# An attention, two networks and their fillers: one PSUM tile for the dummy matmuls, gate logits and held expert work beside the attention

## The chip, the cores and the metric

The kernel runs on one core of a Trainium2 chip. The metric is the device time in microseconds (us), median of several runs. The core's engines run side by side, each through its own list of instructions in order: TensorE (PE; its weight loads are PEld), VectorE (DVE), ScalarE (ACT), GpSimd (POOL) and SyncE (SP), which here issues the DMAs. The order of each list is fixed when the kernel is built; on the chip an instruction waits until its operands and its output's place are free.

## The reference

Three stages follow one another. A linear attention with a state per head (4 batches, 8 heads, 768 tokens, 40 channels):

```python
for t in range(S):
    y[:, :, t] = einsum('bhd,bhde->bhe', rt, state)
    Sa = einsum('bhde,bhe->bhd', state, at)
    state = state * wt[:, :, None, :] - einsum('bhd,bhe->bhde', Sa, bt)
    state = state + einsum('bhd,bhe->bhde', vt, kt)
```

Its output, as x of 3072 tokens by 320, goes through 8 experts with 1024 hidden units, weighted by gates that eight Sinkhorn rounds balance over all tokens:

```python
logits = x @ w_gate
P = exp(logits - logits.max())
for _ in range(8):
    P /= P.sum(1, keepdims=True) + 1e-09
    P /= P.sum(0, keepdims=True) + 1e-09
    P *= N / E
out = sum(P[:, e:e+1] * (maximum(x @ w1[e], 0) @ w2[e]) for e in range(E))
```

A last network follows: `h = maximum(maximum(x @ w1, x @ w2), x @ w3)`, `h @ w_out`. All in float32.

## The kernel before

**Attention.** The 768 tokens are six blocks j of 128; a block and a batch b make one of 24 units n. In a unit, products on PE (`products`, L343) give matrices that VectorE masks (L415) or ScalarE copies (`lab_grams`, L364 and L365). The four `lab` matrices of a block are transposed (L374) and inverted by VectorE and GpSimd (`invert`); `chain` then solves a unit in seven steps (L502, L494), each a group of small matmuls and a copy by ScalarE. `post` forms the output `yps` (L541), updates the state and writes to DRAM (`ydr`). After the fourth unit of a block, `inputs` reads it back as x and splits it into a high and a low part (`split_x`, L198 to L201).

**Fill work.** `fill` puts expert 0's first half of the hidden units beside the attention, for five of the six blocks: four layer-1 blocks of 8 matmuls (f) and four layer-2 blocks of 12 (t), in halves, with the sums sent to DRAM (`part0`). It has one PSUM bank (`psf`), so each block waits for the eviction of the one before. Of the fifth block, the layer-2 blocks t = 2 and 3 are held until the last unit's `post` is done (L618).

**Order.** `drive` writes the order of all engines out by hand when the kernel is built. It takes segments (`Seg`: cost on PE, weight w for its activity, engine that follows, what it needs, a gate) from ten flows, keeps its own clock for each engine, and gives PE the first segment that is ready, or fill work where the attention is behind its pace, or dummies: `idle` issues matmuls of `ones` by `ones` (L690) where PE would have nothing to do, planned at 0.22 us each. Each dummy asks `psf` for a tile of its own, and there is one bank: so each waits for the one before it.

**Networks.** `networks` then runs over 16 pieces (expert, half) and six x blocks, the fifth and sixth block first (`order`). `step` is called between blocks of matmuls, and moves the first of two queues each time: `sides` (here `logits`, which makes the gate logits of all six x blocks, and then `sinkhorn`), and `loads` (here `rest`: weights of piece 1, then five loads of the sums from `part0`; then `rest_x`, the four remaining x blocks).

## Time and profile before

| | |
|---|---|
| Median of 3 runs | 2259.83 us (2259.65 to 2262.43) |
| Profiled execution | 2280.62 us, span 2278.9 us |
| PE busy | 98% of the span |
| VectorE, ScalarE, GpSimd busy | 47%, 27%, 13% |
| Last `yps` of the attention | 647.67 us |
| First matmul of the networks | 663.26 us |

All numbers of the trace come from the profiled execution, which took longer than the median by 20.8 us. In rows of a timeline stand the start, the time until the end, the engine, the line, the operation, output and inputs, and how many records it merges (a float32 matmul makes two); a bracket at the end is the engine's idle time before it and the instruction it waited for. PEclk is the granted clock of TensorE as a share of 2.4 GHz.

### The profile page before, as it was taken

Reading aid. Unit: us, or ns where it says so; the run is one execution under the profiler, and the core shown is the slowest. Engines: PE = TensorE matmul, PEld = TensorE weight load, DVE = VectorE, ACT = ScalarE, POOL = GpSimd, SP = SyncE. Lnnn points to the kernel's source line nnn. Section 1 sums busy time; section 2 is a strip of 40 time slices with the busy share of each in tenths; the row PEclk is TensorE's granted clock in tenths of the full one; section 3 lists DMA queues with packets and bytes.
Section 4 is the critical chain, followed back from the end, with each engine's and each line's share of the span. In section 5 each row is a group of like instructions: output and inputs, shape, how many; then the busy total and the mean of one; then the engine's idle time right before and its main releaser. Section 6 shows DMA issues by size and latency. Waiting matters only on the chain.

```text
span 2278.9 us, 37482 instructions
## 1 busy us (share of the span) xinstructions
PE 2240.8 (98%) x16021; PEld 1965.6 (86%) x16021; DVE 1078.1 (47%) x1882; ACT 608.8 (27%) x1223; POOL 286.6 (13%) x455
## 2 busy tenths in 40 slices
PE   9999999999989999999999999999999999999999
PEld 6787888888867989989989999999999989988888
DVE  5545666654324655555555443333343343442332
ACT  3223544443223133122122121121121121222221
POOL 3242545525000001111100000000000000000000
PEclk9997999999999999999999999999999999999999
DMA  4113343422223011111011000000000000100000
GB/s 114 37 46 103 101 123 84 113 71 87 78 77 122 5 35 48 43 36 51 23 48 52 25 26 13 14 26 13 14 26 8 19 27 7 55 6 24 12 12 25
DMA packets 70980, 105.39 MB, mean 46 GB/s; under 512 B 7341, under 2 KB 51117, under 8 KB 70805
## 3 DMA queue, kind: packets, MB, share of 16 engines
q1 hardware_dynamic: 70805, 102.92, 15.8%
q8 instruction: 127, 2.08, 0.4%
q14 instruction: 48, 0.39, 0.1%
HBM read 87.81 MB, written 15.07 MB: 45 GB/s over the span
## 4 chain that ended last, share of the span: by engine, by line
PE 86%; DVE 1%; DMA 1%; ACT 1%; issue 0%; SPq 0%; ACTq 0%; DVEq 0%
PE ps L223 31%; PE ps L215 29%; PE pu L215 9%; PE psg L343 3%; PE z L502 2%; PE yps L541 2%; PE z L494 2%; PE fps L223 2%; PE fps L215 2%; PE z L470 1%; DMA xr<-ydr 1%; PE dps L556 1%; PE z L454 1%; PE yps L529 1%; PE gps L215 0%
## 5 line engine op out<-in xcount | busy, mean ns | idle before, releaser
L223 PE MATMUL ps<-w2h,h 128*128 128x320 f32 x2912 | 656.3, 309 | 0.0
L223 PEld LDWEIGHTS ps<-w2h,h 128*128 128x128 f32 x2912 | 490.6, 188 | 4.4 <-issue 0.3
L226 ACT ACTIVATE h<-ps 128x512 fp32r<-128x512 f32 x364 | 217.9, 599 | 962.5 <-PE ps L215 955.7
L223 PE MATMUL ps<-w2l,h 128*128 128x320 f32 x1456 | 449.5, 309 | 0.0
L227 DVE SCALAR_TENSOR_TENSOR h<-ps,h 128x512 fp32r<-128x512 f32 x364 | 251.4, 692 | 412.7 <-ACT h L226 411.9
L215 PE MATMUL ps<-xh,w1l 128*128 128x512 f32 x1092 | 314.2, 396 | 8.3 <-DVE xh L201 8.3
L215 PE MATMUL ps<-xh,w1h 128*128 128x512 f32 x1092 | 310.4, 392 | 0.0
L1027 DVE SCALAR_TENSOR_TENSOR acc<-ps,lg,acc 128x320 f32<-128x320 f32 x336 | 184.9, 550 | 256.1 <-PE ps L223 254.6
L223 PEld LDWEIGHTS ps<-w2l,h 128*128 128x128 f32 x1456 | 273.2, 188 | 3.7
L215 PEld LDWEIGHTS ps<-xh,w1h 128*128 128x128 f32 x1092 | 205.7, 188 | 46.2
L215 PEld LDWEIGHTS ps<-xh,w1l 128*128 128x128 f32 x1092 | 201.3, 188 | 47.7 <-DVE xh L201 8.6
L215 PE MATMUL ps<-xl,w1h 128*128 128x512 f32 x728 | 227.4, 394 | 0.0
L215 PE MATMUL pu<-xh,uq 128*128 128x512 f32 x648 | 171.2, 394 | 0.0
L215 PEld LDWEIGHTS ps<-xl,w1h 128*128 128x128 f32 x728 | 137.2, 188 | 32.5
L215 PEld LDWEIGHTS pu<-xh,uq 128*128 128x128 f32 x648 | 120.3, 188 | 25.2
L415 DVE TENSOR_TENSOR gr<-psg,mask 128x512 f32<-128x512 f32 x144 | 92.7, 686 | 80.4 <-PE psg L343 79.8
L396 POOL TENSOR_TENSOR tmp<-lt,tt 128x87 f32<-128x87 f32 (+24 forms) x186 | 105.0, 565 | 174.7 <-DVE lt L374 160.6
L135 POOL TENSOR_TENSOR f<-f,m 128x384 f32<-128x384 f32 (+2 forms) x24 | 24.3, 1014 | 680.3 <-DVE m L133 405.6
L690 PE MATMUL spare<-ones 128*128 128x128 f32 x272 | 101.5, 473 | 8.1 <-DVE ones L81 1.1
L400 POOL TENSOR_TENSOR tt<-tt,tmp 128x87 f32<-128x87 f32 (+24 forms) x186 | 106.8, 574 | 14.6
L690 PEld LDWEIGHTS spare<-ones 128*128 128x128 f32 x272 | 63.9, 291 | 42.1 <-PE spare L690 37.6
L1088 DVE TENSOR_TENSOR g<-pu,g 128x512 f32<-128x512 f32 x72 | 49.8, 692 | 99.9 <-PE pu L215 99.9
(171 smaller groups left out, 2435.9 us busy)
## 6 DMA issues: line engine op xcount, KB each, us to landing
e<-in_em_dram SPq DMA_DIRECT2D x23, 626.0 KB
r<-in_moe_w_dram SPq DMA_DIRECT2D x32, 320.0 KB
r<-in_moe_w_dram SPq DMA_DIRECT2D x32, 256.0 KB
bk<-in_tm_dram SPq DMA_DIRECT2D x24, 320.0 KB
xr<-ydr SPq DMA_DIRECT2D x10, 512.0 KB
kr<-in_em_dram SPq DMA_DIRECT2D x24, 208.0 KB
vt<-in_em_dram SPq DMA_DIRECT2D x24, 208.0 KB
r<-in_em_dram SPq DMA_DIRECT2D x24, 208.0 KB
```

What stands on the lines that cost most here:

```text
L215: nc.tensor.matmul(ps, lhsT=a, rhs=b, start=(n == 0), stop=(n == len(seq) - 1))
L223: nc.tensor.matmul(ps, lhsT=a, rhs=b, start=(n == 0), stop=(n == len(seq) - 1))
L226: nc.scalar.activation(out=h[:, 0], in_=ps, func=AF.Relu)
L227: nc.vector.scalar_tensor_tensor(out=h[:, 1], in0=ps, scalar=0.0, in1=h[:, 0].bitcast(F32), op0=ALU.max, op1=ALU.subtract)
L343: nc.tensor.matmul(ps[a][:, q, :], lhsT=lhs[r, q, :], rhs=rhs[r, q, :], start=(q == 0), stop=True, skip_group_check=True, tile_position=(6 ...
L396: eng.tensor_tensor(out=t, in0=lt[:, m:m + 1, m + 1:32].to_broadcast([128, n, w]), in1=tt[:, 0:n, m:m + 1].to_broadcast([128, n, w]), op=A ...
L400: eng.tensor_tensor(out=tt[:, 0:n, m + 1:32], in0=tt[:, 0:n, m + 1:32], in1=t, op=ALU.subtract)
L415: nc.vector.tensor_tensor(out=t, in0=ps, in1=mask.unsqueeze(1).to_broadcast([C, HP, C]), op=ALU.mult)
L494: nc.tensor.matmul(zh[r, h, 0:D], lhsT=lab[0:32 * i, hx(h), 32 * i - 32:32 * i], rhs=u[0:32 * i, h, 0:D], start=False, stop=True, skip_gro ...
L690: nc.tensor.matmul(ps, lhsT=ones, rhs=ones, start=True, stop=True)
L1027: nc.vector.scalar_tensor_tensor(out=acc[:, i], in0=ps, scalar=pr[:, i, e:e + 1], in1=acc[:, i], op0=ALU.mult, op1=ALU.add,)
L1088: nc.vector.tensor_tensor(out=g, in0=ps, in1=g, op=ALU.max)
```

## The change

1. `idle` asks for a PSUM tile only if it has none (`idler`), and all dummies until the next fill block write to that one.
2. `fill` makes the gate logits of its x block ahead of the layer-1 blocks, in the same bank; `logits` in the networks is left with the sixth x block (the second in `order`). The transposes and the copy of the logits are a function, `turn_logits`.
3. The gate that holds work of the fifth block moves from layer-2 blocks t = 2, 3 to layer-1 blocks f = 2, 3; all layer-2 blocks come after those, so two layer-1 and four layer-2 blocks are held instead of two layer-2 blocks.
4. `rest` loads sums and x blocks in turn (the sums of the first block in `order`, then x and sums of each of the last four), where before all five sums came ahead of the x blocks.

```diff
--- before.py
+++ after.py
@@ -227,6 +227,11 @@
         nc.vector.scalar_tensor_tensor(
             out=h[:, 1], in0=ps, scalar=0.0, in1=h[:, 0].bitcast(F32), op0=ALU.max, op1=ALU.subtract
         )
+
+    def turn_logits(tps, lt, j):
+        for t in range(4):
+            nc.tensor.transpose(tps[:, t, :], lt[:, t * 128:t * 128 + 128], ident[0:NE, 0:NE])
+        nc.vector.tensor_copy(lg[:, 4 * j:4 * j + 4, :], tps)
 
     def load_gate(p):
         wg = p.tile([128, 3, NE], F32, name="wg")
@@ -599,8 +604,19 @@
                 yield Seg(gate=lambda: len(xf) > j)
                 x, x_ = xf[j]
                 hs = []
+                g = Seg(pe=1.87, eng="A", cost=0.65, needs=[bank, x_])
+                yield g
+                idler.clear()
+                ps = psf.tile([NE, TB], F32, tag="f", name="gps")
+                mm_in(ps, *gate, slice(0, NE), x)
+                lt = chp.tile([NE, TB], F32, tag="yt", name="lgt")
+                nc.scalar.activation(out=lt, in_=ps, func=AF.Copy)
+                bank = Seg(pe=0.35, eng="V", cost=0.2, needs=[g])
+                yield bank
+                turn_logits(psf.tile([128, 4, NE], F32, tag="f", name="tps"), lt, j)
                 for f in range(4):
-                    yield Seg(pe=0.92, needs=[bank, x_])
+                    yield Seg(pe=0.92, needs=[bank, x_], gate=lambda: j < NJ - 2 or f < 2 or count["post"] == units)
+                    idler.clear()
                     fs = slice(f * 128, f * 128 + 128)
                     ps = psf.tile([128, TB], F32, tag="f", name="fps")
                     mm_in(ps, ws[0]["h1"], ws[0]["l1"], fs, x, slice(0, 4))
@@ -615,7 +631,8 @@
                     hs.append(h)
                     count["done"] += 1
                 for t in range(4):
-                    yield Seg(pe=0.88, needs=[bank], gate=lambda: j < NJ - 2 or t < 2 or count["post"] == units)
+                    yield Seg(pe=0.88, needs=[bank])
+                    idler.clear()
                     ps = psf.tile([128, TB], F32, tag="f", name="fps")[:, 0:DM]
                     layer2(ps, ws[0]["2"], hs, t, slice(0, 6))
                     spare.append(None)
@@ -686,8 +703,9 @@
         def idle(n):
 
             for _ in range(n):
-                ps = psf.tile([128, 128], F32, tag="f", name="spare")
-                nc.tensor.matmul(ps, lhsT=ones, rhs=ones, start=True, stop=True)
+                if not idler:
+                    idler.append(psf.tile([128, 128], F32, tag="f", name="spare"))
+                nc.tensor.matmul(idler[0], lhsT=ones, rhs=ones, start=True, stop=True)
                 spend(0.22, 1.0)
 
         def behind():
@@ -741,7 +759,7 @@
                     take(f)
 
         with tc.manual_schedule():
-            spare = []
+            spare, idler = [], []
             mask = k0.tile([C, C], F32, name="mask")
             ends = k0.tile([128, WC], F32, name="ends")
             wmid = k0.tile([HR, 1], F32, name="wmid")
@@ -940,7 +958,7 @@
                 yield
 
         def logits():
-            for j in range(NJ):
+            for j in range(1 if begun else 0, 2 if begun else NJ):
                 while len(xs) <= j:
                     yield
                 yield
@@ -950,10 +968,7 @@
                 lt = sm.tile([NE, TB], F32, tag="lt", name="lgt")
                 nc.scalar.activation(out=lt, in_=ps, func=AF.Copy)
                 yield
-                tps = pss.tile([128, 4, NE], F32, tag="s", name="tps")
-                for t in range(4):
-                    nc.tensor.transpose(tps[:, t, :], lt[:, t * 128:t * 128 + 128], ident[0:NE, 0:NE])
-                nc.vector.tensor_copy(lg[:, 4 * order[j]:4 * order[j] + 4, :], tps)
+                turn_logits(pss.tile([128, 4, NE], F32, tag="s", name="tps"), lt, order[j])
 
         pr = lg
 
@@ -1104,18 +1119,25 @@
                 step()
 
         with tc.manual_schedule():
+            def rest():
+                yield from staged(piece(ws[1], wp[1], rp, *pieces[1], "r"), 1)
+                ready.append(1)
+                for k in range(NJ):
+                    if k > 1:
+                        r = fetch_x(rp, order[k])
+                    if k != 1:
+                        nc.sync.dma_start(out=acc[:, 4 * order[k]:4 * order[k] + 4], in_=part0[order[k]])
+                    yield
+                    if k > 1:
+                        for _ in range(3):
+                            yield
+                        xs.append(load_x(xp, r))
+
             def rest_x():
                 yield from staged([
-                    (lambda j=j: fetch_x(rp, order[j]), lambda r, j=j: xs.append(load_x(xp if j or begun else xa, r)))
-                    for j in range(2 if begun else 0, NJ)
+                    (lambda j=j: fetch_x(rp, order[j]), lambda r, j=j: xs.append(load_x(xp if j else xa, r)))
+                    for j in range(NJ)
                 ], 1)
-
-            def rest():
-                yield from staged(piece(ws[1], wp[1], rp, *pieces[1], "r"), 1)
-                for j in order[:1] + order[2:]:
-                    nc.sync.dma_start(out=acc[:, 4 * j:4 * j + 4], in_=part0[j])
-                ready.append(1)
-                yield
 
             ready = []
             if begun:
@@ -1125,7 +1147,7 @@
                 xs = []
                 for load, use in piece(ws[0], wa, rp, *pieces[0], "r"):
                     use(load())
-            loads.append(rest_x())
+                loads.append(rest_x())
             sides.extend((logits(), sinkhorn()))
             prev = None
             last = len(pieces) - 1
```

Rows of the order, as built. First PE at the start of the attention, up to the fifth product of `at` and `bt` (the first of unit 4); `spare` is the dummies' tile, and a name with a number in the brackets is the semaphore of the engine waited for. Before:

```order
L343 MATMUL psg<-at,bt_152 128x128 [waits DVE_49,Activation_49]
L343 MATMUL psg<-at,bt_152 128x128 [waits Activation_49]
L343 MATMUL psg<-at,bt_152 128x128 x6
L690 MATMUL spare<-ones 128x128 [waits PE_49] x9
L343 MATMUL psg<-at,bt 128x128 [waits DVE_49,Activation_49]
L343 MATMUL psg<-at,bt 128x128 [waits Activation_49]
L343 MATMUL psg<-at,bt 128x128 x6
L690 MATMUL spare<-ones 128x128 [waits PE_49] x47
L343 MATMUL psg<-at,bt 128x128 [waits DVE_49,Activation_49]
```

Now:

```order
L348 MATMUL psg<-at,bt_152 128x128 [waits DVE_49,PE_49,Activation_49]
L348 MATMUL psg<-at,bt_152 128x128 [waits PE_49,Activation_49]
L348 MATMUL psg<-at,bt_152 128x128 x6
L708 MATMUL spare<-ones 128x128 x9
L348 MATMUL psg<-at,bt 128x128 [waits DVE_49,PE_49,Activation_49]
L348 MATMUL psg<-at,bt 128x128 [waits PE_49,Activation_49]
L348 MATMUL psg<-at,bt 128x128 x6
L708 MATMUL spare<-ones 128x128 x47
L348 MATMUL psg<-at,bt 128x128 [waits DVE_49,PE_49,Activation_49]
```

The sequence and the counts are the same; the dummies' wait for PE is gone, and the products have one for PE. In the whole program 136 dummies become 167: the first 125 stand in the same places, up to the sixth unit's chain.

Second, PE at the end of the attention, from the last output `yps`; `fps` is the fill's bank, `ps_` that of the networks' first layer-1 block, which reads the sixth x block. Before:

```order
L541 MATMUL yps<-gr,kb 40x128 x8
L223 MATMUL fps<-w2h,fh 128x320
...
L223 MATMUL fps<-w2h,fh 128x320
L690 MATMUL spare<-ones 128x128 x3
L223 MATMUL fps<-w2h,fh 128x320
...
L223 MATMUL fps<-w2h,fh 128x320
L215 MATMUL ps_7028<-xh,w1l 128x512 x3
L215 MATMUL ps_7028<-xl,w1h 128x512 x2
```

Now:

```order
L546 MATMUL yps<-gr,kb 40x128 x8
L215 MATMUL fps<-xh,w1l 128x512 x3
...
L708 MATMUL spare<-ones 128x128 x8
L215 MATMUL fps<-xh,w1l 128x512 x3
...
L708 MATMUL spare<-ones 128x128 x8
L223 MATMUL fps<-w2h,fh 128x320
...
L223 MATMUL fps<-w2h,fh 128x320
L215 MATMUL ps_7017<-xh,w1l 128x512 x3
L708 MATMUL spare<-ones 128x128 x3
L215 MATMUL ps_7017<-xl,w1h 128x512
L223 MATMUL fps<-w2h,fh 128x320
```

Two layer-1 blocks and one layer-2 block now stand ahead of the first matmul on the sixth x block; the other three layer-2 blocks stand between that matmul and its followers, each behind 3 dummies. In the last two units 15 dummies stand where there were 8 (with 3 more, above, behind `yps`).

Third, SP's queue at the change of stage; `part_72` to `part_76` are the sums of blocks 1 to 5, `ydr_66` to `ydr_69` the x of blocks 1 to 4. Before:

```order
L1116 DMA acc<-part_76 128x1280
L1116 DMA acc<-part_72 128x1280
L1116 DMA acc<-part_73 128x1280
L1116 DMA acc<-part_74 128x1280
L1116 DMA acc<-part_75 128x1280
L193 DMA xr<-ydr_66 128x2x512
L194 DMA xr<-ydr_66 64x512
L193 DMA xr<-ydr_67 128x2x512
```

Now:

```order
L1129 DMA acc<-part_76 128x1280
L193 DMA xr<-ydr_66 128x2x512
L194 DMA xr<-ydr_66 64x512
L1129 DMA acc<-part_72 128x1280
L193 DMA xr<-ydr_67 128x2x512
L194 DMA xr<-ydr_67 64x512
L1129 DMA acc<-part_73 128x1280
```

The x of the first block stands behind one load of sums instead of five.

## Rows read from the trace of the kernel before

**Rows 1.** Page, part 1: busy time, share of the span, instructions.
```profile
PE 2240.8 (98%) x16021; PEld 1965.6 (86%) x16021; DVE 1078.1 (47%) x1882; ACT 608.8 (27%) x1223; POOL 286.6 (13%) x455
```

**Rows 2.** Stretches: us, busy of PE, PEld, DVE, ACT, POOL, PEclk, DMA, GB/s.
```profile
94.00:162.00 68.00, 67.31 (x527) 56.32 (x526) 28.53 (x47) 21.56 (x58) 17.46 (x31) 1.00 0.23 58
162.00:231.00 69.00, 65.10 (x791) 55.07 (x790) 41.03 (x69) 27.68 (x69) 20.48 (x34) 0.83 0.36 97
231.00:648.00 417.00, 411.27 (x5639) 359.25 (x5637) 232.78 (x374) 167.01 (x405) 161.37 (x254) 1.00 0.33 91
```

**Rows 3.** Tile of the dummies: ns min/median/max; waits for the dummy before.
```profile
L690 PE MATMUL spare<-ones x272: 275/421/582, 1.1 to 652.6; 128*128 128x128 f32 x136
...
  PE spare L690: 37.6, 111
```

**Rows 4.** Stretches, dummies alone: us, PE and PEld busy, PEclk, DMA.
```profile
0.00:94.00 94.00, 71.58 (x180) 45.15 (x180) 1.00 0.31 77
94.00:162.00 68.00, 14.99 (x39) 9.61 (x38) 1.00 0.23 58
162.00:231.00 69.00, 9.53 (x32) 5.86 (x32) 0.83 0.36 97
```

**Rows 5.** Timeline of PE at the start: start us, us, what, records.
```profile
39.06 2.08 PE L343 MATMUL psg<-at,bt 64*128 64x128 f32 x16
...
56.43 24.69 PE L690 MATMUL spare<-ones 128*128 128x128 f32 x58
...
81.05 2.08 PE L343 MATMUL psg<-at,bt 64*128 64x128 f32 x16
...
89.97 3.47 PE L470 MATMUL z<-v,gr 128*128 128x40 f32 x16
...
93.96 1.27 PE L502 MATMUL z<-zs,td 32*32 32x40 f32 x16
...
114.26 5.06 PE L690 MATMUL spare<-ones 128*128 128x128 f32 x12
```

**Rows 6.** Timeline of DVE, operands of the products at the start.
```profile
15.71 0.69 DVE L329 TENSOR_TENSOR at<-e,p 128x512 f32<-128x512 f32 x1
...
24.55 0.68 DVE L329 TENSOR_TENSOR at<-e,p 128x512 f32<-128x512 f32 x1
...
69.12 0.71 DVE L329 TENSOR_TENSOR at<-e,p 128x512 f32<-128x512 f32 x1
...
72.98 0.68 DVE L428 TENSOR_TENSOR kt<-kr,ip 128x512 f32<-128x512 f32 x1
```

**Rows 7.** Timeline of PE, two products of rows 5 at the faster pace.
```profile
183.79 1.88 PE L470 MATMUL z<-v,gr 128*128 128x40 f32 x16
...
225.88 1.16 PE L343 MATMUL psg<-at,kt 64*128 64x128 f32 x16
```

**Rows 8.** Timeline of ACT, the copy before L502 at 119.3 us.
```profile
114.48 0.43 ACT L498 ACTIVATE zs<-z 32x320 f32<-32x320 f32 x1
```

**Rows 9.** Timeline of PE, end of the attention and start of the networks.
```profile
647.67 1.07 PE L541 MATMUL yps<-gr,kb 128*40 128x128 f32 x16
...
663.26 1.65 PE L215 MATMUL ps<-xh,w1l 128*128 128x512 f32 x3 [8.32 <-DVE xh L201]
...
677.16 0.86 PE L215 MATMUL gps<-xh,gl 128*8 128x512 f32 x3 [1.17 <-DVE lg L956]
...
696.87 1.44 PE L215 MATMUL gps<-xh,gl 128*8 128x512 f32 x3 [5.47 <-DVE xh L201]
```

**Rows 10.** Chain that ended last, same place: start us, us, what.
```profile
652.91 2.04 PE fps L223 x12
...
671.91 1.87 PE gps L215 x8
...
681.05 12.62 DMA xr<-ydr
...
696.87 3.50 PE gps L215 x8
```

## The prediction

> **What bounds the kernel now.** I read the engine shares first: TensorE (PE) is busy for 98% of the profiled span [rows 1]. So only three things can move the end: PE time that is no work, PE idle time, and work done at the lower of TensorE's two clock levels. The table by stretches shows where such time is left. From 231 to 648 us, the attention with expert work beside it, PE is busy for 411 of 417 us at a granted clock of 1.00. From 162 to 231 us the granted clock is 0.83 [rows 2]. Before 162 us the column says 1.00, yet the durations say otherwise: eight products L343 take 2.08 us there and 1.16 us at 226 us, eight products L470 3.47 us at 90 us and 1.88 us at 184 us [rows 5, 7]. I go by the durations: up to about 166 us PE works at 1.2 GHz, later mostly at 2.4 GHz.
>
> Next I looked at the dummies. The view of their tile counts 272 records, two for each of 136 dummies, and 111 waits of a dummy's weight load for the dummy before it, 37.6 us in all [rows 3]. By stretch the dummies hold PE for 71.6, 15.0 and 9.5 us, 96 of 101 us before 231 us [rows 4]. The timeline at the start shows what this does: 47 dummies stand between the product at 39.06 us and that at 81.05 us, 0.85 us each (24.69 us for 29), while VectorE had the operand of the latter ready at 69.8 us [rows 5, 6]. Last I read the change of stage: PE waits 8.3 us for the last x, then 1.2 us and 5.5 us near gate logits [rows 9].
>
> **Part A, the start, up to the first step of the chain (L502, 93.96 us).** With one shared tile a dummy no longer waits for its predecessor (the order loses these waits; the counts up to the sixth unit, 125 dummies, are unchanged). No row shows a 128x128 dummy without the wait. From below I take L470, also a 128x128 stationary operand in two records: 3.47/8 = 0.43 us at the low level, 1.88/8 = 0.235 us at the high one [rows 5, 7]; from above the 0.85 us of today. L470 moves only 40 columns, but it is the nearest row and I take it. At the low level: second product at 16.4 us (operand at 15.71 + 0.69), 2.0 us long; 8 dummies, 3.4 us; third product at 21.9; 9 dummies, 3.9 us; fourth at 27.8 us, not 39.06: 11.3 us earlier, and its operand is there at 25.2 [rows 6]. ScalarE, VectorE and GpSimd follow that product, so the operand at 69.8 comes at 58.5 us. The 47 dummies end at 29.8 + 20.2 = 50.0 us and block nothing; what is late next is VectorE. The product starts at 58.5 instead of 81.05; the next one, on kt, waits 1.0 us for kt (73.66 - 11.3 = 62.4 us). That is 21.5 us, and the 5 dummies before 93.96 give 5 x 0.42 = 2.1: **24 us**. At the high level the fourth product starts at 25.2 us, the products are shorter, and it comes to 29. What rows 3 show is what the Trainium skill describes in "TensorE: Matmul & The Clock Gate", "A second HAM failure mode: psum-queue depth-cycling": going from one PSUM buffer to the next leaves short PE idles, and the clock moves between its levels. The trace agrees with the idles (111 of them); the same page speaks against this change as well, below.
>
> **Part B, from there to 231 us.** 19 dummies stand in 94 to 162 us, 16 in 162 to 231 us. They cost 15.0 and 9.5 us [rows 4]; at 0.43 us each 8.2 and 6.9, at 0.235 us 4.5 and 3.8. That saves 9 to 16 us, and I take 12. These dummies stand where PE waits for the chain, so part of that is lost when they get shorter: before L502 at 119.3 us the six take 5.06 us, but ScalarE's copy is done at 114.9 us, so 4.3 us are pure delay [rows 5, 8]. Then the clock: 67.3 - 15.0 = 52.3 us of PE work runs low in 94 to 162 us [rows 2, 4]; at the high level it would take 1.16/2.08 of that, 23 us less. Nothing shows whether denser dummies lift it; between 0 and 23 I take 10, since PE will now also stand idle between steps. B is **22 us**, bounds 9 and 39.
>
> **Part C, expert work in the attention.** Five of six gate logits go from the network into the attention, each 8 matmuls of 1.87 us [rows 10] and four small transposes; PE is full on both sides, so 9 us leave one and enter the other: 0. If cover is missing, PE waits for ScalarE's copy of them.
>
> **Part D, end of the attention.** The last yps ends at 648.67 us and x is usable at 663.26, 14.6 us later [rows 9]; the chain ydr to xr to split does not change. Before, two layer-2 blocks (2.0 us each [rows 10]) lie in that gap; now the order puts two layer-1 blocks, 16 dummies and one layer-2 block there, and then the matmul that needs x: 5.7 us of work instead of 4.0. PE still waits 14.6 - 5.7 - 16 x 0.235 = 5 us. The other three layer-2 blocks follow with 9 dummies (2.1 us), and 7 more dummies stand in the last two units (1.6 us), where the held work was. 1.7 - 2.1 - 1.6 = **-2 us**.
>
> **Part E, start of the network.** The waits of 1.17 and 5.47 us belong to logits that are gone from here. The second was for the third x, whose DMA took 12.6 us behind five loads of sums on SP's queue [rows 9, 10]; the logits after it took 3.50 us, 1.6 more than at the high level. SP now has one load of sums ahead of that x, and PE needs it only after more than 40 us of other matmuls: 8.2 us go. The Sinkhorn starts at once behind the last logits, and three small PE instructions wait for VectorE with everything queued behind them. Nearest row: 1.17 us each, 3.5 us (bounds 0 and 8). **+5 us**.
>
> **Sum.** 24 + 22 - 2 + 5 = 49 us. The profiled execution took 2280.6 us (span 2278.9), so its like would take 2232. The median of the runs is 2259.8, 20.8 less. Taking the extra as spread evenly, the forecast is 2259.8 - 49 = **2211 us**. If it lay wholly in the stretch before 231 us, the gain would be 28 and the time 2232.
>
> **Rivals.**
> 1. The clock rises early and stays up: A 29, B 39, so 29 + 39 - 2 + 5 = 71 us and 2189 us. For it: back-to-back dummies are dense work, and the matmuls that follow one another from 663 us on start at 1.65 us for three and are at 1.87 us for eight 9 us later [rows 9, 10]. Against: PE will idle from 50.0 to 58.5 us. The Trainium skill, "TensorE: Matmul & The Clock Gate", "What's actually happening", has activity release the throttle, which is this case.
> 2. The clock stays low to 162 us and the chain's own waits (ScalarE's copies, kr's loads) take most of the dummies' place: A 24, B 2, D and E 3: 29 us, 2231 us. For it: after idles of 8.3 and 5.5 us the trace has PE slow each time [rows 9]. The same page, "HAM oscillation — how this bites in real kernels", says idle gaps between bursts put PE back to the low clock: a rule against a change that shortens fillers. By it B's clock part is 0.
> 3. A dummy still waits for the last write to its tile: A and B are 0, and +3 is left: 2257 us. Against: the waits are gone from the order.
> 4. Slower: PE falls to the low level between 231 and 648 us, because a logits block holds the only spare bank through two copies and the fills come too late. Each us of high-level work would take 0.79 us more (2.08/1.16); from 49/0.79 = 62 us of the 411 on, the gain is eaten, and at a quarter, 103 us, the time is 2259.8 - 49 + 81 = 2292 us. For it: 0.83 in 162 to 231 us. Against: 1.00 over all of the stretch, which gets more work [rows 2].
>
> **How the numbers follow.** Forecast 0.58, rivals 0.16, 0.18, 0.04, 0.04. The forecast's own range is 2198 to 2227, B's bounds mostly. To leave out no more than 2 in 10 the range takes most of rivals 1 and 2: 2188 to 2238. What this kernel's measurement tells from no change is about 0.2% (4.5 us): faster than that 0.92, within it 0.04, slower 0.04.
>
> **What would show it.** Right: dummies of 0.5 us or less at the start; the fifth product of at and bt near 58 us with VectorE as its releaser; the first L502 chain step (now L507) near 70 us; no 5.5 us wait behind the network's first layer 2; about 5 us of wait for the last x. Wrong: dummies of 0.85 us; PE busy short of 95% with the attention's end not earlier than 625 us; a granted clock under 0.9 after 231 us.

## The result, and the profile of the changed kernel

| | before | changed |
|---|---|---|
| Median | 2260.07 us (2259.65 to 2262.43, 4 runs) | 2232.46 us (2231.34 to 2233.89, 4 runs) |
| Ratio, 95% interval | | 0.9876 [0.9859, 0.9893] |
| Profiled execution | 2280.62 us | 2231.34 us |
| The same pair later, beside the experiments | 2264.09 us (17 runs) | 2230.87 us (6 runs), 0.9846 [0.9802, 0.9891] |

The change gains 27.6 us by the medians. The two profiled executions lie 49.3 us apart, because the profiled execution of before was a long one. Rows of the changed kernel follow the order of the rows of before; its lines behind L229 are 5 to 18 numbers later (L507 was L502, L475 L470, L348 L343, L315 L310, L708 L690).

The page's busy line, the answer to [rows 1]:

```profile
PE 2172.6 (97%) x16083; PEld 1930.9 (87%) x16083; DVE 1082.4 (49%) x1882; ACT 609.5 (27%) x1223; POOL 284.0 (13%) x455
```

PE has 68 us less busy time with 31 more dummies. The stretches of [rows 2], same columns:

```profile
94.00:162.00 68.00, 62.68 (x784) 53.74 (x781) 39.17 (x64) 27.11 (x69) 39.36 (x62) 0.77 0.37 95
162.00:231.00 69.00, 65.84 (x898) 56.34 (x898) 50.80 (x81) 28.12 (x68) 33.66 (x49) 0.96 0.39 106
231.00:648.00 417.00, 403.72 (x5204) 347.03 (x5203) 211.52 (x339) 155.87 (x368) 123.84 (x208) 0.98 0.30 84
```

PE runs 784 matmul records between 94 and 162 us where it ran 527. The tile of the dummies, [rows 3], durations in ns:

```profile
L708 PE MATMUL spare<-ones x334: 273/275/583, 1.1 to 634.3; 128*128 128x128 f32 x167
...
  DVE fh L227: 6.5, 4
```

No wait of a dummy for a dummy is left (there were 111); the 6.5 us are new and come up below. The dummies alone, by the stretches of [rows 4]:

```profile
0.00:94.00 94.00, 31.72 (x210) 29.28 (x210) 0.78 0.37 94
94.00:162.00 68.00, 6.80 (x30) 4.96 (x30) 0.77 0.37 95
162.00:231.00 69.00, 1.65 (x10) 1.26 (x10) 0.96 0.39 106
```

40 us instead of 96. PE's timeline at the start, [rows 5]:

```profile
25.37 1.25 PE L348 MATMUL psg<-at,bt 64*128 64x128 f32 x16 [0.96 <-DVE at L334]
26.55 10.76 PE L708 MATMUL spare<-ones 128*128 128x128 f32 x94
55.37 2.17 PE L348 MATMUL psg<-at,bt 64*128 64x128 f32 x16 [18.06 <-DVE at L334]
...
63.17 3.47 PE L475 MATMUL z<-v,gr 128*128 128x40 f32 x16
...
67.16 1.27 PE L507 MATMUL z<-zs,td 32*32 32x40 f32 x16
...
158.85 1.14 PE L459 MATMUL z<-s,at 104*128 104x104 f32 x8
```

The 47 dummies take 10.76 us, 0.23 us each, instead of 40 us; VectorE releases the product at 55.37 us; the chain's first step stands at 67.16 us instead of 93.96. The last row is the first product of unit 4, a mark used below: it came at 207.67 us before.

The end of the attention and the start of the networks, [rows 9]:

```profile
611.71 1.07 PE L546 MATMUL yps<-gr,kb 128*40 128x128 f32 x16
...
616.24 2.05 PE L708 MATMUL spare<-ones 128*128 128x128 f32 x16 [1.41 <-DVE fh L227]
...
621.88 2.05 PE L708 MATMUL spare<-ones 128*128 128x128 f32 x16 [1.41 <-DVE fh L227]
...
645.20 0.27 PE L980 MATMUL t<-ident,m 128*1 128x128 f32 x1 [1.65 <-DVE m L977]
646.03 0.58 PE L986 MATMUL t<-m,ones 1*128 1x1 f32 x2 [0.56 <-DVE m L983]
```

The waits of 8.32, 1.17 and 5.47 us are gone. Two batches of eight dummies stand behind waits of 1.41 us for the only spare bank, and the Sinkhorn brings two waits of its own. One wait is new in the middle. VectorE's timeline, then PE's:

```profile
114.79 0.84 DVE L315 TENSOR_SCALAR e<-e 128x512 f32<-128x512 f32 x1 [5.38 <-DMA e<-in_em_dram]
```

```profile
120.94 1.67 PE L546 MATMUL yps<-gr,kb 128*40 128x128 f32 x8 [3.19 <-DVE gr L420]
...
133.99 1.27 PE L507 MATMUL z<-zs,td 32*32 32x40 f32 x16 [1.32 <-ACT zs L503]
```

PE's granted clock around it (us, PE busy, PEclk, DMA, GB/s):

```profile
110.00:120.00 10.00, 7.69 (x138) 1.00 0.51 122
120.00:130.00 10.00, 9.06 (x92) 0.66 0.51 130
130.00:140.00 10.00, 7.93 (x75) 0.70 0.36 101
140.00:150.00 10.00, 10.00 (x113) 0.50 0.27 66
```

VectorE's list is in order, so the wait for a load holds back the state update and the masked products behind it; PE stands idle for them, and then works mostly at 1.2 GHz up to about 158 us. From 127 to 134 us its steps are at the high level again; the second fall comes with a wait of 1.32 us for ScalarE's copy. The faster kernel has run into its loads: before, the same instruction (unit 9's) waited 1.11 us, at 159.16 us.

**Where the time went.** Each execution is cut at three marks: the chain's first step, unit 4's first product, the start of the last `yps`. Most of the experiments stand here too (us, all from PE's timeline and the span):

| kernel | to first step | to unit 4 | to last `yps` | rest |
|---|---|---|---|---|
| before | 93.96 | 113.71 | 440.00 | 1631.2 |
| before, profiled again | 93.96 | 104.48 | 439.26 | 1630.5 |
| changed | 67.16 | 91.69 | 452.86 | 1617.9 |
| changed, again | 67.14 | 94.65 | 451.88 | 1619.8 |
| shared tile only | 67.13 | 91.60 | 442.18 | 1627.6 |
| all but the shared tile | 75.93 | 105.96 | 454.76 | 1624.2 |
| changed, no dummy issued | 66.72 | 95.21 | 452.69 | 1612.9 |
| before, 35 dummies fewer | 76.26 | 113.66 | 450.91 | 1628.0 |
| shared tile late only | 93.97 | 91.57 | 439.13 | 1629.1 |
| shared tile early only | 67.23 | 101.90 | 447.35 | 1630.3 |
| changed, end trimmed | 67.45 | 91.71 | 448.68 | 1616.1 |
| trimmed, one load counted longer | 65.56 | 76.61 | 456.87 | 1616.6 |
| trimmed, seven loads counted longer | 67.17 | 73.83 | 450.11 | 1616.3 |

Between the two profiled executions the first two columns carry the gain: 26.8 and 22.0 us. The last two exchange about 13 us with each other. The two rows that start at about 76 us have a tile for each dummy at the start, as before; they come up below.

### The profile page after: what moved, and what is told of

Same layout as the page of the kernel before. It is cut to its first block, busy times and chain, and to the rows that moved or that the text cites. A ratio compares the mean times of both kernels' runs of the same rounds, so it can differ in the third digit from the quotient of the medians.

```text
span 2229.6 us, 37611 instructions
## 1 busy us (share of the span) xinstructions
PE 2172.6 (97%) x16083; PEld 1930.9 (87%) x16083; DVE 1082.4 (49%) x1882; ACT 609.5 (27%) x1223; POOL 284.0 (13%) x455
## 4 chain that ended last, share of the span: by engine, by line
PE 89%; ACT 1%; DVE 1%; DMA 0%; issue 0%; SPq 0%; ACTq 0%
PE ps L223 32%; PE ps L215 30%; PE pu L215 9%; PE psg L348 3%; PE z L507 2%; PE yps L546 2%; PE fps L215 2%; PE z L499 2%; PE fps L223 2%; PE z L475 1%; PE dps L561 1%; PE z L459 1%; ACT ld L369 1%; PE yps L534 1%; PE spare L708 1%; PE tp L439 0%
## 5 line engine op out<-in xcount | busy, mean ns | idle before, releaser
L215 PEld LDWEIGHTS ps<-xh,w1l 128*128 128x128 f32 x1092 | 200.9, 188 | 38.5
L507 PEld LDWEIGHTS z<-zs,td 32*32 32x32 f32 x1536 | 63.6, 111 | 23.2 <-issue 9.7
L507 PE MATMUL z<-zs,td 32*32 32x40 f32 x1536 | 75.4, 202 | 5.5 <-ACT zs L503 5.4
```

The costliest lines, as they stand in the source:

```text
L215: nc.tensor.matmul(ps, lhsT=a, rhs=b, start=(n == 0), stop=(n == len(seq) - 1))
L507: nc.tensor.matmul(zh[r, h, 0:D], lhsT=td[r, 8 * b + hx(h), :], rhs=zs[r, h, :], start=(h == 0), stop=True, skip_group_check=True, tile_po ...
```

## The experiments

**The kernel before, once more.** No edit.

> The kernel before, unchanged, for a second profile and the clocks of its runs. Its profiled execution took 2280.6 us, its runs 2260, and the changed kernel gained 49 us between the profiled executions but 28 between the medians. Theory (the extra 20.8 us lie in the start): a profile near 2260 shows the first chain step of the fifth unit (L502) near 200 us instead of 220.5, and the stretch from there to the end unchanged. Rival (spread evenly): 220.5 and all later stretches 1% shorter.

2269.7 us (10 runs) beside 2270.8 (23 runs of before); ratio 1.0015 [0.998, 1.005]. Its profiled execution took 2269.87 us, 10.75 less than the first one, and 9.2 of that lies between the first step and unit 4 (second column). The granted clock of this one:

```profile
160.00:180.00 20.00, 18.62 (x268) 0.97 0.34 91
180.00:200.00 20.00, 19.13 (x236) 0.77 0.36 92
```

In the first profile the rows of these stretches read 0.78 and 0.71. All steps stand at the same times up to 150 us; then the clock rises, at about 155 us here and 168 us there, by the durations of the steps. The fifth unit's first step comes at 211.3 us, and the rest is as long as before: as the theory has it, though the profile lies 10 us from 2260. So one program differs from run to run by when its clock rises; 17 runs of before on one chip reach from 2251 to 2283 us.

**The shared tile alone.** The kernel before with `idler` and nothing else (shown in part; `idler.clear()` stands ahead of each fill block):

```diff
...
+                if not idler:
+                    idler.append(psf.tile([128, 128], F32, tag="f", name="spare"))
+                nc.tensor.matmul(idler[0], lhsT=ones, rhs=ones, start=True, stop=True)
```

> The kernel before with the shared dummy tile alone; fill, logits and loads as before. Theory (the dummies' waits were the cost, parts D and E are worth about 3): 2233 to 2240 us, 20 to 27 of the 28 us gained, first chain step near 67 us. Rival (the end of the attention and the start of the networks carry the gain): 2248 to 2256 us.

2229.69 us (6 runs), ratio 0.9828 [0.9778, 0.9878]. Within the intervals this is all of the change's gain.

**All but the shared tile.** The changed kernel with a tile for each dummy:

```diff
-                if not idler:
-                    idler.append(psf.tile([128, 128], F32, tag="f", name="spare"))
-                nc.tensor.matmul(idler[0], lhsT=ones, rhs=ones, start=True, stop=True)
+                ps = psf.tile([128, 128], F32, tag="f", name="spare")
+                nc.tensor.matmul(ps, lhsT=ones, rhs=ones, start=True, stop=True)
```

> The changed kernel with a tile of its own for each dummy, as before: logits beside the attention, held work and loads in turn are kept. Theory: 2254 to 2262 us, since the start is as before and D and E together are near +3 (more dummies at the end of the attention now wait for one another). Rival: 2235 to 2245 us.

2268.71 us (12 runs), ratio 1.0011 [0.9978, 1.0043]: nothing. But the start is not as before in this profile:

```profile
32.94 1.16 PE L348 MATMUL psg<-at,bt 64*128 64x128 f32 x16
34.03 25.64 PE L707 MATMUL spare<-ones 128*128 128x128 f32 x94
...
75.93 1.27 PE L507 MATMUL z<-zs,td 32*32 32x40 f32 x16
```

The steps turn fast at about 23 us, among dummies that wait for one another; the 47 dummies take 0.55 us each, and the chain starts 18.0 us earlier than in either profile of before. The dummies of this stretch stand as before, on a tile each, so the edit is no likely reason for it: executions with waiting dummies differ at the start too, by the clock. Later the clock is up from 84 to 91 us and then down to about 145 us.

Against the shared tile alone, the changed kernel's third column is 10.7 us longer and its last 9.7 shorter. By PE's busy time 10 us of logits go into the third column and 8 us of held fill work out of it into the last; dummies, waits and the clock make up the rest.

**No dummy issued.** The changed kernel as planned, with no dummy matmul issued:

```diff
-                if not idler:
-                    idler.append(psf.tile([128, 128], F32, tag="f", name="spare"))
-                nc.tensor.matmul(idler[0], lhsT=ones, rhs=ones, start=True, stop=True)
```

> The changed kernel with no dummy issued: they are planned, so the order of all else is the same, and left out. Theory (they hold nothing up any more and keep the clock higher in part): slower than the changed kernel by 5 to 15 us, near 2243, first chain step at about 68 to 70 us and products at 2.08 us up to the fifth unit. Rival (dummies now only cost time): 2215 to 2228 us.

2235.57 us (4 runs), ratio 0.9863 [0.9801, 0.9924], which the changed kernel's ratio can't be told from. Two of its chain steps:

```profile
94.88 1.27 PE L507 MATMUL z<-zs,td 32*32 32x40 f32 x16
...
101.09 0.76 PE L507 MATMUL z<-zs,td 32*32 32x40 f32 x16
```

From about 100 us on they take 0.76 us, the time at the high level, without any dummies, until the clock falls at 120 us as it does in the changed kernel. In the profiles of before they take 1.27 us up to some 155 and 168 us, and with all but the shared tile, in the same order, the granted clock is 0.50 from 100 to 140 us. So in these profiles dummies on a tile each did not merely fail to lift the clock: the rise that lasts came some 45 to 68 us later with them than with none. Neither theory has the time.

**35 of the 47 dummies left out.** The kernel before; the 12 left are on a tile each:

```diff
...
+                if count["lab"] != 4 or count["pre"]:
                     ps = psf.tile([128, 128], F32, tag="f", name="spare")
                     nc.tensor.matmul(ps, lhsT=ones, rhs=ones, start=True, stop=True)
```

> The kernel before, with 35 of the 47 dummies that stand ahead of the fifth product not issued (12 are left, each on its own tile); nothing else is changed and nothing is left out of the result. Theory A (the dummies cost time only because each waits for the one ahead of it, and so stand between ready work and PE): the 12 end near 50 us, the product of 81.05 us starts when VectorE is done (69.8 us, its producer itself held by the product of 39.06 us), so the first step of the chain comes 11 us earlier (83 us) and the run 8 to 14 us under the kernel before. Theory B (the gain of the shared tile is that dense dummies lift the clock): without these dummies the clock has less reason to rise, the chain starts at or after 93.96 us and the time is that of before within 5 us. If the first step comes 11 us earlier and the time does not follow, what is gained at the start is given back by a later rise of the clock.

2268.19 us (12 runs), ratio 1.0007 [0.9979, 1.0036]. The start obeys theory A; the time is theory B's:

```profile
33.23 1.16 PE L343 MATMUL psg<-at,bt 64*128 64x128 f32 x16
...
63.18 2.08 PE L343 MATMUL psg<-at,bt 64*128 64x128 f32 x16 [22.37 <-DVE at L329]
...
76.26 1.27 PE L502 MATMUL z<-zs,td 32*32 32x40 f32 x16
...
330.06 0.41 PE L541 MATMUL yps<-gr,kb 128*40 128x128 f32 x2 [1.72 <-DVE gr L415]
```

The chain starts 17.7 us earlier. But 5.8 us of that are there ahead of the dummies left out: the fourth product comes at 33.23 us instead of 39.06, since the clock was up from about 23 us in this execution, as with all but the shared tile. That is luck of this execution; the other 11.9 us are the 11 of theory A. Against the second profile of before, its second column is 9.2 us longer (the clock is at 0.50 to 150 us, 74 us behind the first step, where that profile took 61) and its third 11.7 us. The clock behind the wait of 1.72 us:

```profile
330.00:340.00 10.00, 9.76 (x112) 0.54 0.27 66
340.00:350.00 10.00, 10.00 (x74) 0.50 0.01 3
350.00:360.00 10.00, 10.00 (x86) 0.76 0.37 107
```

That is 24 us at 1.2 GHz ((0.46 + 0.50 + 0.24) x 10 x 2), or 24 x (1 - 1.16/2.08) = 10.6 us lost. In this profile the earlier start is given back where the clock stays down longer. That is one profile; the twelve runs (2255 to 2273 us) say only that there is no gain.

**The shared tile late, and early.** The kernel before with the shared tile for the dummies behind unit 0's first stage only, and for those ahead of it only (the edit against the shared tile alone):

```diff
-                if not idler:
+                if not idler or not count["pre"]:      # late; early: or count["pre"]
+                    idler.clear()
```

> The kernel before, in which only the dummies planned from the end of unit 0's first stage on (from about 92 us of the profile of before on: 14 batches before 231 us and all later ones) share a tile; the 85 or so ahead of it stay on a tile each. Theory 1 (the clock of the chain decides: dummies that wait for one another keep it low between 94 and 160 us, and the 27 us at the start are worth little by themselves): the chain still starts at 92 to 94 us, but it runs at the high level from about 120 us on, and 15 to 35 us of the 36 to 41 us are kept (2225 to 2250, ratio 0.985 to 0.993). Theory 2 (as predicted: the start carries 24 to 27 us and the rest about 10): 5 to 12 us under before, ratio 0.995 to 0.998.

2246.81 us (12 runs), ratio 0.9908 [0.9879, 0.9937], which is 20.9 us of 2269.4 [14 to 27].

```profile
93.97 1.27 PE L502 MATMUL z<-zs,td 32*32 32x40 f32 x16
...
107.85 0.76 PE L502 MATMUL z<-zs,td 32*32 32x40 f32 x16 [0.75 <-ACT zs L498]
```

The start is as before to 0.01 us, and two steps later the chain runs at the high level. The second column shrinks to 91.57, the value of the changed kernel.

> The other half: only the dummies ahead of the end of unit 0's first stage share a tile, the later ones have a tile each. The chain starts near 67 us, as in the changed kernel. Theory 1 (the clock decides): it then runs at the low level up to 130 us or more and most of the 27 us are lost again, as where 35 of the 47 dummies were left out: 0 to 12 us under before (ratio 0.995 to 1.0). Theory 2 (the start carries it): 24 to 30 us under before, ratio 0.987 to 0.99.

2247.28 us (12 runs), ratio 0.9931 [0.9902, 0.996], which is 15.7 us [9 to 22]. The steps run low for longer again:

```profile
104.67 1.27 PE L502 MATMUL z<-zs,td 32*32 32x40 f32 x16
110.47 0.76 PE L502 MATMUL z<-zs,td 32*32 32x40 f32 x16
...
308.83 0.41 PE L541 MATMUL yps<-gr,kb 128*40 128x128 f32 x2 [1.68 <-DVE gr L415]
```

The start is 26.7 us earlier than in the profiles of before, and about 16 us are gained. The wait of 1.68 us is followed by 20 us at the low level in this profile, and the third column is 8.1 us longer than in the second profile of before; but the other runs of before may have started earlier than its two profiles (see the end), and then there was less to gain. The halves add up: 20.9 + 15.7 = 36.6 us, where the shared tile alone gave 39.1 [28 to 50] and the changed kernel 34.9 [25 to 45]. The late half came out as theory 1 had it; the early half lies between the two theories. Beside the same runs of before the two medians are 0.5 us apart, so which half is worth more is not shown.

**The changed kernel again**, beside the runs with fewer dummies, denser ones and a trimmed end.

> The changed kernel unchanged, beside the others on one chip. If the shared tile carries all of the change and the other parts are worth nothing, it is within 6 us of what the kernel before with the shared tile alone showed against before (ratio 0.983, 0.978 to 0.988). If the profiled pair (gain 49 us) is the rule, the ratio is 0.978 or less; if the medians of the first runs (gain 27.6 us) are, 0.988.

2230.87 us (6 runs), ratio 0.9846 [0.9802, 0.9891]: as the shared tile alone, within its interval.

**Denser dummies.** In the changed kernel, 2 and 3 matmuls by turns for 35 of the 47 planned dummies ahead of the fifth product (shown in part):

```diff
+                for i in range(1 if count["lab"] != 4 or count["pre"] else 2 + count["extra"] % 2):
                     nc.tensor.matmul(idler[0], lhsT=ones, rhs=ones, start=True, stop=True)
```

> The changed kernel, with 2.5 times as many dummies in the stretch ahead of the fifth product (they end near 54 us instead of 37.3, VectorE's operand comes at 55.4), so that PE no longer stands idle for 18 us before it. Theory (the idle 18 us put the clock back to the low level): products 5 and 6 take 1.2 us instead of 2.17 and the first chain steps run high, 4 to 15 us less than the changed kernel. Rival (the clock of the stretch up to 160 us is set by the waits within the chain): the products are faster by 2 us and nothing else moves; the time is that of the changed kernel within 3 us.

2232.67 us (6 runs), ratio 0.9854 [0.981, 0.990]: no gain. The condition leaves 12 of the 47 as they were, so there are 99 dummies and not 2.5 times 47; they end near 49 us instead of 54, PE still idled 6.5 us and the product that follows is still slow:

```profile
27.02 22.38 PE L709 MATMUL spare<-ones 128*128 128x128 f32 x198
55.86 2.17 PE L348 MATMUL psg<-at,bt 64*128 64x128 f32 x16 [6.46 <-DVE at L334]
```

So this run does not tell what a start at the high level would be worth.

**The end trimmed.** The changed kernel without the dummies behind the last unit, and with more turns in the Sinkhorn:

```diff
+                if count["post"] == units:
+                    spend(0.22, 1.0)
+                    continue
...
+            for _ in range(3):      # ahead of t1; one turn more ahead of t2 and of each ct
+                yield
```

> The changed kernel, with the dummies planned behind the last unit of the attention not issued and 2 to 3 more turns ahead of the three small PE instructions of the Sinkhorn. Theory: in the changed kernel 2 x 2.07 us (8 dummies each, behind the release of their bank, so pure delay), up to 3 x 0.76 us of dummies among the held work, and 1.65 + 0.56 + 0.25 us of Sinkhorn waits are PE time that nothing needs: 4 to 9 us less than the changed kernel (it may give 2 us back, since PE then waits for the last x). Rival: the clock falls for want of dummies and the gain is gone: same time, with matmuls at the low level behind 616 us.

2224.49 us (6 runs), ratio 0.9826 [0.9778, 0.9873]; 6 us under the changed kernel beside it, though the two ranges overlap (2220 to 2235, 2228 to 2236). In the profile the two batches of 2.05 us are gone; the turns did not help:

```profile
635.55 0.27 PE L984 MATMUL t<-ident,m 128*1 128x128 f32 x1 [1.65 <-DVE m L980]
639.57 0.58 PE L991 MATMUL t<-m,ones 1*128 1x1 f32 x2 [3.75 <-DVE m L987]
```

The second wait grew from 0.56 to 3.75 us. The cause stays open.

**The load of e counted longer.** The trimmed kernel; `drive` takes 3 us more for the load that VectorE waited for (shown without the trimming):

```diff
+                    if k == 2 * NB + 1:
+                        ready[k] = Seg(done=ready[k].done + 3.0)
```

> The changed kernel without the dummies behind the last unit and with more turns in the Sinkhorn (as in the trimmed run, 6 us under the changed kernel), and with one number of the planner's changed: it counts 3 us more for the load of e for unit 9, so that VectorE's state update of unit 1 and two products with the mask stand ahead of the instruction that waits 5.4 us for that load. Theory: this wait on VectorE's queue is what makes PE stand idle for 3.1 us at 121 us, and with that the clock falls until 150 us: without it 3 us of wait go and up to 13 us of low clock: 6 to 16 us under the trimmed run, ratio to before 0.975 to 0.980. Rival (PE then waits some us later for something else and the clock falls all the same): within 4 us of the trimmed run, ratio 0.981 to 0.985.

2215.80 us (6 runs), ratio 0.9795 [0.9755, 0.9835]. VectorE now does unit 1's state update and two masked products first, and the wait of 5.4 us is 0.2:

```profile
112.39 0.74 DVE L315 TENSOR_SCALAR e<-e 128x512 f32<-128x512 f32 x1 [0.20 <-DMA e<-in_em_dram]
127.85 0.43 DVE L315 TENSOR_SCALAR e<-e 128x512 f32<-128x512 f32 x1 [2.47 <-DMA e<-in_em_dram]
```

PE's clock around it:

```profile
120.00:130.00 10.00, 9.51 (x148) 1.00 0.74 200
130.00:140.00 10.00, 8.69 (x100) 0.74 0.26 65
140.00:150.00 10.00, 10.00 (x73) 0.50 0.42 123
```

The fall comes some 13 us later, behind the load for the next unit. In the table the stretch up to unit 4 is 15 us shorter than in the trimmed run, and the third column 8 us longer. The intervals of the two ratios overlap (0.9826 [0.9778, 0.9873] for the trimmed run), so a gain in time against it is not shown. So I counted all loads of units 9 to 15 longer (`2 * NB + 1 <= k < 4 * NB`).

> As the last run, but the planner counts 3 us more for the loads of e of units 9 to 15, not of unit 9 alone. In the last run the load for unit 10 became the next wait: VectorE waited 2.5 us for it at 127.9 us, PE 1.1 us at 134.4 us, and the clock fell there until about 155 us. Theory: with this wait gone too the clock stays up through 155 us: another 5 to 10 us, ratio to before 0.971 to 0.978. Rival (each such wait has another behind it: ScalarE's copies or the mask products stop PE at 130 to 145 us all the same): within 4 us of the last run, ratio 0.978 to 0.982.

2216.74 us (6 runs), ratio 0.9807 [0.9771, 0.9843]. The profile shows what the theory said,

```profile
130.00:140.00 10.00, 9.86 (x175) 1.00 0.21 59
140.00:150.00 10.00, 10.00 (x148) 1.00 0.69 194
150.00:160.00 10.00, 9.52 (x156) 1.00 0.18 44
```

and the last `yps` starts at 591.11 us (599.04 in the run before it, 607.84 in the trimmed one). The median does not follow: it is within 1 us of the run before it (on another chip; the ratios agree as well), and the profiled execution (2209.1 us) was the fastest of the six. By the medians these two are the fastest kernels of the study.

## Why the prediction was right, and where it was off

**What bounds the kernel.** Right. The dummies that wait for one another and the low clock are what the change took out; all the rest of it moved the time by nothing that can be told from 0 (-0.2 to +0.4%).

**The sum.** 49 us forecast, 49.3 between the two profiled executions: 26.8 for part A (24), 22.0 for part B (22), and 0.5 for the rest (3). That match is partly luck: from the second profile of before it is 38.5 us. The median lies outside the forecast's own 2198 to 2227, near rival 2's 2231, which has another mechanism. The 0.2% taken as what a measurement can tell was too fine: the intervals of the experiments reach 0.3 to 0.6% to either side.

**The step that failed** is the last one, from the profiled execution to the median: "Taking the extra as spread evenly, the forecast is 2259.8 - 49". As far as the profiles show it, the extra lay in the stretch whose cost the change removes: 9.2 of the 10.75 us between the two profiles of before do. The other reading that the text gave, "If it lay wholly in the stretch before 231 us, the gain would be 28 and the time 2232", gives what was measured: 27.6 us, 2232.46. B's 22 us were taken from an execution whose clock had risen late; from the second profile of before B is 12.8. From a start like that of all but the shared tile, A would be 75.93 - 67.16 = 8.8. No profile of before near its median was taken, so how the 20.8 us divide stays open.

**Part A.** Right in mechanism, and nearly in size against the profile that it was read from. The dummies took about 0.43 us at the low level (14 in 5.8 us at the start of the changed kernel's second profile, the clock up for the last of them) and 0.23 at the high one, as L470 had suggested. That row moves 40 columns and a dummy 128; why the two agree no row shows. The clock rose during the first batches, which puts A between its two cases (24 and 29). VectorE releases the fifth product, as said. What I had not seen is that the start of before is no fixed 93.96 us, and that an earlier start by itself gave about 16 us, and nothing in the run with 35 dummies fewer.

**Part B.** Right in size against the first profile (22.0; 12.8 against the second), wrong about how. I put 12 us on shorter dummies and 10 on the clock, and asked whether denser dummies lift it. The run with none issued shows that dummies need not lift it at all: with them gone the chain's own matmuls bring it up by 100 us. With the chain's dummies sharing a tile it first comes up at 63 to 103 us in the profiles; on a tile each, the rise that lasts came at 145 us or later in four of five, and at 108 us in the early-sharing run. The late-sharing run shows the worth of this half by itself, 14 to 27 us. The Trainium skill, "TensorE: Matmul & The Clock Gate", "A second HAM failure mode: psum-queue depth-cycling", says that going through PSUM banks leaves short idles which make the clock swing. The trace agrees on the waits (111, 37.6 us). The profiles of before show no swing up to 155 and 168 us, but a clock that stays low; with all but the shared tile it does swing, up at about 23, 84 and 145 us and down in between. That the waits hold it down is argued from the runs in which they are gone, not read from a row.

**Rival 2, the chain's own waits.** Half right. The wait ahead of the first fall was not one of those named (ScalarE's copies, kr's loads) but a load of e at the head of VectorE's list; ahead of the second, at 134 us, it was ScalarE's copy (1.32 us). From 121 to about 158 us the clock is mostly down. With the load counted longer, the wait went and the fall came later. The Trainium skill, "TensorE: Matmul & The Clock Gate", "HAM oscillation — how this bites in real kernels", has idle gaps put PE back to the low clock. The trace agrees: 3.19 us idle, then low.

**Part C.** Right: the five logits take 10.1 us of PE in the attention and 11.6 us less in the networks, where one batch had run at the low level.

**Parts D and E.** Forecast -2 and +5, together +3. The last two columns together gained 0.5, a balance of larger terms that the forecast did not have. Apart from the logits, 8 us of held fill work moved from the third column into the last. PE's idle time in the last fell from 21.8 to 10.6 us, and its dummies rose by 5.4; in the third the idle time rose from 7.8 to 11.3 us and the mean clock fell from 0.99 to 0.98. The details differ as well. PE never waits for the last x. In the order I had counted 16 dummies of 0.235 us as cover for that wait; they need the bank that the layer-1 block holds, so they stand behind its release (1.41 us), take 2.05 us, and x is there when they end. The trimmed run, without them, is 6 us faster, with ranges that overlap. The Sinkhorn's waits are 2.2 us instead of the 3.5 I took.

**Rivals 1, 3 and 4** did not come about: the clock rises early but falls again at 121 us; no dummy waits for a dummy; the granted clock is 0.98 from 231 to 648 us.

## What to carry to other kernels

A filler must not wait for another filler: give all of them one PSUM tile, then ask whether any are needed, since here none issued was as good. Before a saving is taken off the median, see which stretch made the profiled execution differ from it; if it is the one that the change removes, part of the saving isn't there. Where executions of one program differ by 18 us at their start, one profile is no baseline. When a stage gets faster, look for loads that stand at the head of an in-order list: the next wait is there.

## What the runs showed that I had not expected

- The granted clock reads 1.00 in the profile of before up to 170 us, where it first falls, while up to 162 us eight products take 2.08 us instead of 1.16: neither the low level nor the rise shows in it. Durations tell the level there, and a higher mean clock over the span doesn't mean a faster run.
- The same wait of PE for VectorE's masked product is followed by very different stretches at the low level. Before:

```profile
347.15 0.41 PE L541 MATMUL yps<-gr,kb 128*40 128x128 f32 x2 [1.68 <-DVE gr L415]
```

Behind it 3.4 us run low (0.93 and 0.90 in the two stretches of 10 us); behind the wait of 1.68 us in the early-sharing run 20 us, behind the 1.72 us of the run with fewer dummies 24. What decides between them is not in the rows, and stays open. It makes 8 to 11 us of difference, and with the time at which the clock first rises it would account for much of the 32 us over which the runs of before are spread on one chip.

- The start differs between executions as long as the early dummies wait for one another: the first step of the chain stands at 94 us in three profiles and at about 76 us in two. With those dummies on one tile, or none issued, it stands at 65.6 to 67.5 us in all nine. The mean clock that each run lists is a mark of this: it is 0.987 to 0.993 in the four profiles whose first rise came at about 100 us or later, and 0.975 and 0.963 in the two that rose at 23 us. Of the 74 runs of before beside the experiments 20 list 0.985 or more, with a median of 2272.9 us, and 54 list less, with 2261.2. So most runs of before probably started their chain early, unlike both of its profiles; they left no traces, and this is not shown.
